# Where streamed weight tiles begin in their ring places: the 33 that began at the first byte now begin 192 bytes in

## The chip, the cores and the metric

The kernel runs on one core of one Trainium2 chip. The metric is the device time of one execution in microseconds (us); smaller is better. A trace of one execution, taken by the hardware profiler, stands beside the times.

## What is computed

A linear attention with an RMS norm, followed by a two-layer feed-forward net with an exact GELU, all in float32:

```python
kv  = einsum('bhsd,bhse->bhde', k, v)          # batch 8, heads 8, seq 576, head_dim 64
out = einsum('bhsd,bhde->bhse', q, kv)
x   = out / sqrt(mean(out*out, -1) + 1e-6) * g_norm     # then [4608 tokens, 512]
h   = x @ w_in                                  # 512 -> 2048
g   = 0.5 * h * (1 + erf(h / sqrt(2)))
y   = g @ w_out                                 # 2048 -> 512
```

## The kernel before

**Chunks.** The 4608 tokens are worked off in nine chunks `c` of 512. Chunks 0 and 1 are computed plainly (`layer1`, lines 665, and `layer2`, line 692). Chunks 2 to 8, about three quarters of the time, use a scheme with seven block products in place of eight (Winograd's form of Strassen's) for both layers; everything below is about these. Each float32 operand is split into a high and a low float32r part, and a product of 128 columns of weights is three TensorE instructions: high by high, low by high, high by low.

**Layer 1 of a chunk** (`product`, line 554). The chunk has eight column groups `j`, each with a first part (block products `k` = 0 to 3) and a second part (`k` = 4, 5, 6). One block product is 6 instructions. The weights are the stationary operand (loaded into the array by a weight load), the activations `x` the moving one, 256 columns wide. A weight tile holds two block products, so it serves 12 instructions. There are 336 instructions in layer 1 of a chunk. **Layer 2** (`Fast.matmuls`, line 1241) is 28 ticks `(k, n)` of 12 instructions, with the roles turned round: the weights move, the split GELU outputs are stationary.

**What interrupts layer 1.** TensorE's order is written out by hand. Between the parts of layer 1 it also works for the next chunk: the projections of the attention (line 241, `project_pair`), a folding of the squares (line 293, `fold`) and the sums over keys (line 188, `sum_kv`). In chunk 2 the projections come after the second parts of `j` = 0 and of `j` = 1. In chunks 3 to 7 they come after the first part of `j` = 0. The fold comes after the second part of `j` = 2, and in chunks 3 to 5 the sum over keys after the second part of `j` = 5 (in chunk 2 it lies in layer 2). After each of these interruptions layer 1 goes on with the first part of the next column group, whose first weight tile is `("in", j, 0)`. Chunk 8 has no next chunk and no interruption.

**The ring.** The split weight tiles of the scheme lie in HBM (`products`), 128 x 1024 float32 = 512 KB each. 301 uses of them over chunks 2 to 8 form a `queue`; the tiles that stay in SBUF (`RESIDENT`) are not in it. `fetch(n)` issues the DMA of the n-th use on SP's queue (line 507) into one of six places in turn, `RING` = `w_in0, 1, 2, 3, 10, 11`; `used` issues fetch n + 6 when TensorE has done with use n.

**Where a tile begins in its place.** A place is 4096 bytes a partition for the tile and 256 bytes more (`EXTRA`), so a tile can begin at the first byte or further in. `AWAY` is 48 float32 = 192 bytes. All tiles that stay in SBUF begin at `AWAY`. Of the ring's tiles, those for which `aligned` says yes begin at the first byte and all others at `AWAY`:

```python
away = 0 if aligned(*queue[n]) else AWAY
ring[n] = kept[i][:, away:away + 2 * DM]
```

Every SBUF tile from `x0` on (the moving operands `x`, the GELU outputs, the ring, the work tiles) has a size that is a multiple of 256 bytes, and they are allocated one behind the other. So all of them begin at the same remainder of 256 bytes: a ring tile at its first byte begins at the remainder of the operand that it is multiplied with, a tile at `AWAY` does not. Operands inside a tile begin at multiples of 512 bytes from its begin.

`aligned` says yes 33 times: in every chunk for the first tick of layer 2, `TICKS[0]`; for `("in", j, 0)` with `j` = 0, 2, 3, 4 in chunks 2 and 8, `j` = 0, 1, 4, 7 in chunks 3 to 5, `j` = 0, 1, 4 in chunks 6 and 7. In the words of the last paragraph but two: for the first tile of each layer, and for the first tile after each interruption of layer 1, but for the one in chunk 2 ahead of `j` = 1, where the last of layer 2 of chunk 1 (line 692) comes between; in chunk 8 the same four `j` as in chunk 2 are named.

Of the kernel before, what the change touches and what calls it, by code (L numbers as in the profile page):

```python
# [23 lines left out]
FAST = PLAIN  # L24
# [13 lines left out]
def linear_attn_rms_gelu_ffn(  # L38
# [18 lines left out]
    NT, DM = out.shape  # L57
    B, NP = kv_main.shape[:2]
# [5 lines left out]
    NCH = NT // CH  # L64
# [28 lines left out]
    AWAY = 3 * LINE  # L93
# [81 lines left out]
    def rows(r):  # L175
        return slice(r * D, (r + 1) * D)
# [209 lines left out]
    kept = {}  # L386

    def reused(i, dtype=F32):

        if i not in kept:  # L390
            kept[i] = block_tile(f"w_in{i}", dtype)
        return kept[i][:, :2 * DM]
# [77 lines left out]
    TICKS = [(0, 0), (0, 1), (0, 2), (2, 0), (2, 1), (0, 3), (2, 2), (2, 3)]  # L470
# [20 lines left out]
    queue = []  # L491
# [5 lines left out]
    ring = {}  # L497

    def fetch(n):

        if n < len(queue):
            key = queue[n][1]
            i = RING[n % len(RING)]
            reused(i, F32R)
            away = 0 if aligned(*queue[n]) else AWAY
            ring[n] = kept[i][:, away:away + 2 * DM]
            nc.sync.dma_start(out=ring[n].bitcast(F32), in_=products[key])

    def aligned(c, key):

        kind, j, k = key
        if kind == "out":
            return (j, k) == TICKS[0]
        if k:
            return False
        if c > FAST and c + 1 < NCH:
            return j in ((0, 1, 4, 7) if c + 2 < B else (0, 1, 4))
        return j in (0, 2, 3, 4)

    def operand(c, key):  # L520
        at = c, key
# [2 lines left out]
    def used(c, key):  # L524
        if (c, key) in place:
            n = place[c, key]
            ring.pop(n)
            fetch(n + len(RING))
# [254 lines left out]
    for d in range(0, 2 * D, BLK):  # L783
        h = d // D * D
        nc.gpsimd.tensor_tensor(
            out=fold[:, d:d + BLK], in0=ident[:, h:h + BLK], in1=ident[:, h + BLK:h + 2 * BLK],
# [27 lines left out]
    def sum_squares(n):  # L814
# [12 lines left out]
        out=half_g, in0=ps[:, :1], scalar1=0.5, scalar2=None, op0=ALU.mult  # L827
# [3 lines left out]
        out=sums[:, :P], lhsT=ones, rhs=eps, start=True, stop=False,  # L831
# [4 lines left out]
        out=root_g, in0=half_g, scalar1=D ** 0.5, scalar2=None, op0=ALU.mult  # L836
# [9 lines left out]
    for half in range(2):  # L846
# [6 lines left out]
        out=sums[:, :n_fold].rearrange("p (g b) -> p g b", g=2), lhsT=fold,  # L853
# [3 lines left out]
    for half in range(2):  # L857
        nc.scalar.activation(
            out=first.block((1, half)),
# [8 lines left out]
    for half in range(2):  # L868
# [3 lines left out]
            out=first.o_all[:, half], in0=first.ps.pop((0, half)), scalar=root_g, in1=bc,  # L872
            op0=ALU.mult, op1=ALU.mult,
        )
        n = 2 + half
        bc = bank(f"acc{n}")
        for t in range(NG):
            for h in range(2):
                at = column(n, t) + h
                nc.tensor.matmul(  # L880
                    out=bc[rows(h), t * P:(t + 1) * P],
# [173 lines left out]
    def later(c, i):  # L1055

        if i == 7:
            sums[c] = attn[c + 1].fold()
        if i in (5, 7):
            load_kv(c + 2, (i - 5) // 2)  # L1060
        if i == 9:
            attn[c + 2].load(0)
        if i == 10:
            attn[c + 2].load(1)
        if i in (5, 7):
            raw_out(6 + i // 7)
        if i == 15:
            place_kv(c + 2, range(NP))
        send()
        for n in {9: (0, 1), 14: (2, 3), 15: (4, 5)}.get(i, ()):  # L1070
            fetch(n)
        for n in {6: (0,), 9: (1,), 12: (2,), 14: (3,)}.get(i, ()):
            keep(RESIDENT[n])
# [43 lines left out]
    for s in range(PLAIN * NF):  # L1117
        c, i = divmod(s, NF)
# [5 lines left out]
        if c == 0:  # L1124
# [25 lines left out]
            for _ in range(2):  # L1150
                if i > 6 and RAW:
                    store_raw, j = RAW.pop(0)
# [8 lines left out]
        else:  # L1161
            spread_matmuls(c, i)
            g[s] = gelu(h.pop(s))
            nxt, k = attn[c + 1], SQUARES.index(i) if i in SQUARES else None
# [189 lines left out]
    for c in range(FAST, NCH):  # L1354
# [4 lines left out]
        for j, second in parts_of_layer1():  # L1359
# [26 lines left out]
            if waiting and (last or (j, second) != (waiting[0], True)):  # L1386
                n = waiting.pop(0) // 2
# [65 lines left out]
```

## Time and profile before

| | before |
|---|---|
| three runs | 776.0, 776.16, 777.76 us (median 776.16) |
| span of the profiled execution, first to last instruction | 774.5 us |
| TensorE (PE) busy | 767.6 us, 99% |
| VectorE (DVE), ScalarE (ACT), GpSimd (POOL) busy | 578.8, 360.4, 157.7 us |
| DMA | 244.89 MB, mean 316 GB/s |
| PE's granted clock | 0.999 |

The span is one execution under the profiler; the run's median lies 1.66 us above it, for what comes ahead of the first and behind the last instruction. In the lists of the profile, PE is a matmul instruction and PEld the weight load that goes with it. Matmuls overlap, since one is recorded as longer than the distance to the next, so a group's time is best taken from the start of its first instruction to the start of the next group's first. "x12" after a group is its number of instructions.

### The profile page before, as it was taken

To read this page: it belongs to the slowest core of one execution; us is meant where nothing else is said; L and a number is where in the kernel's file an instruction comes from. 1 tells how busy PE (TensorE), PEld (TensorE's weight loads), DVE (VectorE), ACT (ScalarE), POOL (GpSimd) and SP (SyncE) were. 2 spreads that over 40 slices of the span, in tenths; PEclk is the share of its full clock that TensorE was granted. 3 is DMA by queue.
4 is the path that set the end of the run, shared out by engine and by line. 5 is a ranking of instruction groups with operands and counts; after the bars stand their busy time and mean duration, and the time that the engine had idled before them with its cause. 6 is when DMAs were issued, how large, how long until landed. Compare 5 with 4: busy or idle time off the path is not lost.

```text
span 774.5 us, 16764 instructions
## 1 busy us (share of the span) xinstructions
PE 767.6 (99%) x6598; PEld 726.5 (94%) x6598; DVE 578.8 (75%) x1057; ACT 360.4 (47%) x689; POOL 157.7 (20%) x141
## 2 busy tenths in 40 slices
PE   8999999999999999999999999999999999999998
PEld 6888888888899999999999999999999999999998
DVE  3999987899668974789477947694689568964683
ACT  3777645534363644364334724462436353632460
POOL 1000145423527000610043002500160016001100
PEclk9999999999999999999999999999999999999999
DMA  9997966797999999979998999989898989799974
GB/s 343 406 408 255 334 227 227 241 357 263 337 312 353 374 339 348 372 266 353 349 356 298 320 376 332 335 276 346 306 328 281 346 302 325 243 329 339 331 244 168
DMA packets 89602, 244.89 MB, mean 316 GB/s; under 512 B 8884, under 2 KB 30900, under 8 KB 89524
## 3 DMA queue, kind: packets, MB, share of 16 engines
q1 hardware_dynamic: 89520, 243.83, 87.9%
q8 instruction: 52, 0.85, 0.4%
q14 instruction: 26, 0.21, 0.1%
q10 hardware_dynamic: 4, 0.00, 0.0%
HBM read 207.09 MB, written 34.08 MB: 311 GB/s over the span
## 4 chain that ended last, share of the span: by engine, by line
PE 95%; DMA 2%; DVE 2%; ACT 0%; SPq 0%; issue 0%
PE acc L1241 23%; PE acc L554 22%; PE h L554 13%; PE acc L692 11%; PE h L665 11%; PE a L1241 10%; PE a L188 2%; PE a L241 1%; DMA kv_main<-kv_main 1%; PE h L655 1%; DMA w_in<-qT 1%; PE acc L241 1%; DVE x L1219 1%; PE acc L880 0%; PE a L293 0%; DVE x L1208 0%
## 5 line engine op out<-in xcount | busy, mean ns | idle before, releaser
L665 PE MATMUL h<-x,w_in 128*128 128x512 f32 x360 | 87.0, 390 | 0.0
L665 PEld LDWEIGHTS h<-x,w_in 128*128 128x128 f32 x360 | 67.3, 188 | 14.4 <-ACT w_in L641 0.3
L692 PE MATMUL acc<-w_out,gh 128*128 128x512 f32 x256 | 79.6, 392 | 0.0
L554 PE MATMUL acc<-w_in,w_in 128*128 128x256 f32 x480 | 64.7, 278 | 0.0
L554 PEld LDWEIGHTS acc<-w_in,w_in 128*128 128x128 f32 x480 | 59.1, 188 | 0.3 <-issue 0.2
L692 PEld LDWEIGHTS acc<-w_out,gh 128*128 128x128 f32 x256 | 47.5, 188 | 10.2 <-issue 0.3
L554 PE MATMUL acc<-x,w_in 128*128 128x256 f32 x390 | 52.8, 279 | 0.0
L545 DVE TENSOR_TENSOR gl<-acc,gh 128x256 f32<-128x256 f32 (+1 forms) x77 | 34.4, 446 | 24.2 <-ACT gh L567 18.5
L692 PE MATMUL acc<-w_out,gl 128*128 128x512 f32 x128 | 49.8, 389 | 0.0
L554 PEld LDWEIGHTS acc<-x,w_in 128*128 128x128 f32 x390 | 48.1, 188 | 1.0 <-issue 0.8
L678 ACT ACTIVATE gh<-h 128x512 fp32r<-128x512 f32 x32 | 19.2, 599 | 63.0 <-PE h L665 63.0
L1241 PE MATMUL acc<-w_in,w_in 128*128 128x256 f32 x372 | 46.7, 277 | 0.0
L567 ACT COPY gh<-h 128x256 f32<-128x256 f32 x21 | 7.8, 369 | 81.7 <-PE h L554 81.7
L1241 PEld LDWEIGHTS acc<-w_in,w_in 128*128 128x128 f32 x372 | 44.4, 188 | 0.0
L1208 POOL TENSOR_TENSOR w_in<-w_in,w_in 128x512 f32<-128x512 f32 x5 | 6.5, 1298 | 181.5 <-ACT w_in L586 181.5
L1241 PE MATMUL acc<-w_in,x 128*128 128x256 f32 x324 | 40.6, 277 | 0.0
L334 POOL TENSOR_TENSOR o<-o,sq 128x512 f32<-128x512 f32 x24 | 33.3, 1386 | 35.2 <-DVE sq L338 34.3
L586 ACT ACTIVATE w_in<-acc 128x512 f32<-128x512 f32 x32 | 19.2, 599 | 44.0 <-DVE acc L545 44.0
L554 PE MATMUL h<-w_in,w_in 128*128 128x256 f32 x288 | 38.7, 277 | 0.0
L1241 PEld LDWEIGHTS acc<-w_in,x 128*128 128x128 f32 x324 | 38.6, 188 | 0.1
L283 DVE TRANSPOSE_TENSOR_REDUCE part<-sq 128x16 f32<-128x512 f32 x33 | 23.4, 708 | 17.1 <-ACT sq L273 17.1
L554 PEld LDWEIGHTS h<-w_in,w_in 128*128 128x128 f32 x288 | 35.5, 188 | 0.0
(302 smaller groups left out, 1911.2 us busy)
## 6 DMA issues: line engine op xcount, KB each, us to landing
w_in<-products_in SPq DMA_DIRECT2D x168, 512.0 KB, 5.3
w_in<-products_out SPq DMA_DIRECT2D x133, 512.0 KB, 5.1
products_in<-w_in SPq DMA_DIRECT2D x40, 256.0 KB, 3.9
w_in<-w_in SPq DMA_DIRECT2D x16, 512.0 KB, 10.2
kv_main<-kv_main SPq DMA_DIRECT2D x16, 512.0 KB, 6.4
w_out<-w_out SPq DMA_DIRECT2D x16, 512.0 KB, 10.2
q<-qT SPq DMA_DIRECT2D x15, 512.0 KB, 6.5
products_out<-w_out SPq DMA_DIRECT2D x23, 256.0 KB, 3.9
```

Of the source, the lines that this page charges most:

```text
L188: nc.tensor.matmul(out=ps[r, n * D:(n + 1) * D], lhsT=k[:, r], rhs=v[:, r], start=(j == 0), stop=(j == NJ),)
L241: nc.tensor.matmul(out=ps[rows(h), p % 2 * HALF + a:p % 2 * HALF + e], lhsT=kv[b % 2][rows(half), p, h ^ half], rhs=q[rows(half), h, a:e], ...
L283: nc.vector.tensor_reduce(out=self.part[:, 2 * k[0] + k[1], :], in_=sq.rearrange("p (b d) -> p b d", d=BLK), op=ALU.add, axis=AX.X, apply_ ...
L334: eng.tensor_tensor(out=o, in0=o, in1=bc, op=ALU.mult)
L545: return eng.tensor_tensor(out=out, in0=x, in1=y, op=op)
L554: nc.tensor.matmul(out=out, lhsT=y, rhs=x[:, z, kb], start=first and kb + i == 0, stop=kb == 1 and i == 2, skip_group_check=True,)
L567: nc.scalar.copy(out=u[:, left], in_=a[:, left])
L586: nc.scalar.activation(out=grid(t)[:, :, j % 2], in_=ps.rearrange("p (a n) -> p a n", a=2), func=AF.Gelu)
L665: nc.tensor.matmul(out=h, lhsT=parts["in", i][:, w][:, p * P:(p + 1) * P], rhs=at.x[p][:, x], start=(m + p == 0), stop=(m == 2 and p == NP ...
L678: nc.scalar.activation(out=gh, in_=h, func=AF.Gelu)
L692: nc.tensor.matmul(out=ps, lhsT=x[:, ts], rhs=parts["out", i][:, w], start=(i == 0 and m == 0), stop=(m == 2 and (i == NF - 1 or (i, t) == ...
L1241: nc.tensor.matmul(out=self.bank[name][a][:, a * HALF:(a + 1) * HALF], lhsT=x[:, at], rhs=y, start=(k in (0, 2, 1) and n + p + m == 0 and ...
```

## The change

All tiles of the ring begin at `AWAY`; the function `aligned` goes. The 33 transfers write, and the 396 instructions that read them (26 tiles in layer 1, 7 in layer 2, 12 each) read, 192 bytes further on. The order of instructions and their waits are the same on all engines; no instruction and no byte is added or taken away.

```diff
             key = queue[n][1]
             i = RING[n % len(RING)]
             reused(i, F32R)
-            away = 0 if aligned(*queue[n]) else AWAY
-            ring[n] = kept[i][:, away:away + 2 * DM]
+            ring[n] = kept[i][:, AWAY:AWAY + 2 * DM]
             nc.sync.dma_start(out=ring[n].bitcast(F32), in_=products[key])
-
-    def aligned(c, key):
-
-        kind, j, k = key
-        if kind == "out":
-            return (j, k) == TICKS[0]
-        if k:
-            return False
-        if c > FAST and c + 1 < NCH:
-            return j in ((0, 1, 4, 7) if c + 2 < B else (0, 1, 4))
-        return j in (0, 2, 3, 4)
```

## The prediction

> **What bounds the kernel now.** I read the page first, then the waits of TensorE, then its timeline where the seven-product chunks run.
>
> ```profile
> span 774.5 us, 16764 instructions
> PE   8999999999999999999999999999999999999998
> PEclk9999999999999999999999999999999999999999
> PE 95%; DMA 2%; DVE 2%; ACT 0%; SPq 0%; issue 0%
> ```
>
> TensorE is busy in every slice at an even clock, and 95% of the chain that ended last is its own work. Its waits, for the stretch from 207 to 771 us that holds chunks 2 to 8, come to one row:
>
> ```profile
> PE acc L1241 <- DVE x L1219: 0.2, 1, 0.2
> ```
>
> So TensorE waits for no weight tile, and the transfers have room: fetches are held back by TensorE, which has to free their places, not the reverse (below: the DMA queue's largest waits, then the landing times of line 507 as min/median/max).
>
> ```profile
> SPq L507 <- PE acc L554: 139.4, 105, 4.4
> ...
> DMA to landing us min/median/max: 3.0/5.2/8.2
> ```
>
> What is left is the distance from one matmul to the next. It isn't the same everywhere. This is the timeline of PE in layer 1 of chunk 2 (start, length, engine, line, operation):
>
> ```profile
> 212.34 0.39 PE L692 MATMUL acc<-w_out,gl 128*128 128x512 f32 x1
> 212.57 1.58 PE L554 MATMUL acc<-x,w_in 128*128 128x256 f32 x12
> 213.98 1.58 PE L554 MATMUL acc<-w_in,w_in 128*128 128x256 f32 x12
> 215.40 1.57 PE L554 MATMUL h<-w_in,w_in 128*128 128x256 f32 x12
> 216.81 0.86 PE L554 MATMUL h<-w_in,w_out 128*128 128x256 f32 x6
> 217.61 1.10 PE L241 MATMUL a<-q,kv 64*64 64x192 f32 x24
> 218.63 1.69 PE L554 MATMUL acc<-x,w_in 128*128 128x256 f32 x12
> 220.16 2.88 PE L554 MATMUL acc<-w_in,w_in 128*128 128x256 f32 x24
> 222.88 0.84 PE L554 MATMUL acc<-w_in,w_out 128*128 128x256 f32 x6
> ```
>
> From 220.16 to 222.88 us 24 matmuls take 2.72 us, 113.3 ns each; all their weights lie at 192 bytes. From 212.57 to 216.81 us 36 matmuls take 4.24 us, 117.8 ns each, and **their weights lie at 192 bytes too**. Between the two stand the projections and, at 218.63, a tile that begins at the first byte. The recorded durations (min/median/max) show the same three cases: first the stretch from 212.5 us, then that from 218.6 us.
>
> ```profile
> L554 PE MATMUL acc<-x,w_in x12: 279/279/280, 212.6 to 213.9; 128*128 128x256 f32 x12
> ...
> L554 PE MATMUL acc<-x,w_in x12: 278/282/386, 218.6 to 220.0; 128*128 128x256 f32 x12
> L554 PE MATMUL acc<-w_in,w_in x12: 276/276/276, 220.2 to 221.4; 128*128 128x256 f32 x12
> ```
>
> 276 ns belongs to the pace of 113.3 ns, 279 to 117.8, 282 to 283 to a tile at the first byte. What a tile at the first byte costs without an interruption ahead of it stands in chunk 8, which has none:
>
> ```profile
> 702.11 0.88 PE L554 MATMUL acc<-w_in,w_in 128*128 128x256 f32 x6
> 702.83 0.88 PE L554 MATMUL acc<-s,w_in 128*128 128x256 f32 x6
> 703.55 1.52 PE L554 MATMUL acc<-w_in,w_in 128*128 128x256 f32 x12
> ```
>
> 12 matmuls in 1.44 us, 120 ns each.
>
> So I read the trace thus: with weights at 192 bytes, layer 1 has two steady paces, 113.3 and 117.8 ns, and keeps the one that it is in: 42 matmuls in a row stayed slow, over four tiles. A tile at the first byte is slower than both, but the tile behind it comes out at 113.3. That is seen after all 26 such tiles of layer 1.
>
> **The change part by part.** No instruction, byte or wait moves; the terms are paces alone.
>
> *What it takes away.* A group of 12 at 120 ns instead of 113.3 is 12 x 6.7 ns = 0.08 us. I take that for the 7 of layer 2. Of the 26 in layer 1 most stand behind an interruption and start below 120 (at 218.63 the least is 278 and the median 282, not 283), so they are worth between 0.05 and 0.08 us; I take 0.065. For layer 2 the tile behind it also recovers slowly:
>
> ```profile
> 250.99 1.60 PE L1241 MATMUL acc<-w_in,w_in 128*128 128x256 f32 x12
> 252.43 1.54 PE L1241 MATMUL acc<-w_in,s 128*128 128x256 f32 x12
> 253.81 0.39 PE L1241 MATMUL acc<-r,x 128*128 128x256 f32 x2
> ```
>
> 1.44 us, then 1.38 where 12 x 113.3 is 1.36: 0.02 more, seven times. Together 26 x 0.065 + 7 x 0.08 + 0.14 = 2.4 us. This is the most that the change can gain.
>
> *What it may bring.* The tile at the first byte is also what stood behind each interruption of layer 1. Without it, the question is which pace layer 1 falls into there. The trace has one entry into layer 1 with no such tile, at 212.57, and it fell into 117.8. All the others have one. The bounds for each stretch from an interruption to the next are therefore 113.3 (all as after a first-byte tile) and 117.8 ns (as at 212.57). I take 117.8: it is the only row with the same weights, the same roles and no first-byte tile, though the work ahead of it was line 692 and not 241, 293 or 188. The stretches, by line 554 alone (length, PE busy, instructions; a count of 127 or 187 has one in it that ends there), are two of chunk 2 and its last, the three of chunk 3, two of chunk 7, and all of chunk 8:
>
> ```profile
> 218.62:223.64 5.02, 5.01 (x42) 1.00 0.90 322
> 224.68:229.62 4.94, 4.93 (x42) 1.00 0.85 284
> 229.75:250.98 21.23, 21.23 (x187) 1.00 0.95 344
> 297.18:311.64 14.46, 14.46 (x126) 1.00 0.86 317
> 311.77:326.29 14.52, 14.52 (x127) 1.00 1.00 369
> 328.78:335.75 6.97, 6.96 (x60) 1.00 0.76 251
> 620.56:635.02 14.46, 14.46 (x126) 1.00 0.85 292
> 635.15:656.38 21.23, 21.23 (x187) 1.00 0.93 325
> 694.56:732.94 38.38, 38.37 (x336) 1.00 0.92 336
> ```
>
> A stretch of n matmuls at 117.8 gains 12 x 2.2 = 0.03 us on the old first tile and loses (n - 12) x 4.5 ns on the rest. For n = 42 that is +0.11 us, for 60 +0.19, for 126 +0.49, for 186 +0.76. Chunk 2: 0.11 + 0.11 + 0.76 = 0.98. Chunks 3 to 5: (0.49 + 0.49 + 0.19) x 3 = 3.5. Chunks 6 and 7: (0.49 + 0.76) x 2 = 2.5. Sum +7.0 us.
>
> *Where a layer begins without an interruption.* Here the roles of the operands turn, and for one step a weight load and a moving operand lie at the same remainder, as inside a first-byte tile. In layer 2 the pace of 113.3 looks like the only one: it came back within a tile after 250.99, and also after an interruption with no first-byte tile, at 271.90:
>
> ```profile
> 271.28 0.69 PE L188 MATMUL a<-w_in 112*64 112x64 f32 x17
> 271.90 1.65 PE L1241 MATMUL acc<-w_in,x 128*128 128x256 f32 x12
> 273.38 1.52 PE L1241 MATMUL acc<-w_in,w_out 128*128 128x256 f32 x12
> 274.74 0.50 PE L1241 MATMUL acc<-w_out,w_out 128*128 128x256 f32 x3
> ```
>
> 1.48 us including the restart, then 1.36. So layer 2 saves its 0.56 + 0.14 = 0.70 us. For the begin of layer 1 (seven times) no row shows the case; a step at the same remainder is what led to 113.3 each time, so I take 113.3. With the three other tiles of chunk 8, ten tiles of layer 1 then save 10 x 0.065 = 0.65 us. If instead the begin falls into 117.8, chunks 3 to 7 lose little (24 matmuls to the first interruption, about 0.04 us each), but chunk 8 keeps it for 336 matmuls: 324 x 4.5 - 12 x 2.2 - 3 x 12 x 6.7 = 1.2 us lost instead of 0.3 gained.
>
> *Sum.* +7.0 - 0.70 - 0.65 = +5.65 us on the span of 774.5. The runs' median stands 1.66 us above the span, which the change doesn't touch: 776.16 + 5.65 = 781.8.
>
> *The row against the skill.* In the Trainium skill, the page "SBUF — State Buffer", section "Who interferes with whom", gives TensorE two independent read ports, one for the moving operand and one for weight loads, and says "PE and ACT never wait on anyone". By that rule 192 bytes would change no pace and the sum would be zero. The rows above disagree: 276 and 283 ns for the same instruction with the same operands' sizes, by the tile's begin.
>
> **The rivals.** A difference of 0.3%, 2.3 us, is about what a measurement of this kernel can tell from no change.
>
> 1. *Clean restart.* The slow stretch at 212.57 comes from line 692 ahead of it, and after lines 241, 293 and 188 layer 1 goes straight to 113.3, as layer 2 did at 271.90. Then only the first term is left: -2.4 us, 773.8. It decides at the first matmuls after each interruption. For it speaks the layer 2 row; against it that layer 2 recovered from everything and layer 1 stayed slow for 42 matmuls. Chance 0.13.
> 2. *Layer 1 slow from its begin as well*, chunk 8 above all: 1.5 us for chunk 8 and about 0.1 for each of six begins on top of the forecast, 784.0. No row shows this entry. Chance 0.22.
> 3. *Only one or two kinds of interruption lead to 117.8.* The projections' stretches (two of chunk 2, one in each of five chunks) are worth 0.22 + 5 x 0.49 = 2.7 us, the fold's 0.76 + 3 x 0.49 + 2 x 0.76 = 3.7, the sums' 0.6. With one of the two large ones alone, against the gains of 1.35 and of the clean stretches of some 0.6: +0.7 to +1.9 us, 776.9 to 778.1; the fold with the sums, or a slow pace that gets lost halfway, lie at 777 to 779. Chance 0.13.
> 4. *Layer 2 slow too*: (336 - 12) x 4.5 ns = 1.46 us in six chunks and some 0.7 in chunk 2, with the 0.70 not saved, on top of the forecast: 792. The recoveries at 252.43 and 271.90 speak against it. Chance 0.05.
> 5. *The begin is not what sets the pace.* If the 283 ns went with what runs beside these groups (DVE, DMA) and not with the address, nothing changes: 776.2. The groups at 702.11 have no interruption ahead of them and read other operands than those at 218.63, so little speaks for it. It is also what the Trainium skill's rule quoted above would give. Chance 0.04.
>
> **How the numbers follow.** The forecast has 0.43. Slower by over 0.3% are the forecast, rivals 2 and 4, and the upper part of 3 (0.06 of 0.13): 0.76. Within 0.3% are rival 5, the rest of 3 and half of rival 1, which ends right at the bound: 0.04 + 0.07 + 0.07 = 0.18. Faster is the other half of 1: 0.06. The range leaves out rivals 1 and 4 (0.18) and takes in 3 from its lower end and 2: 776.0 to 785.0, with 1 us above rival 2 for the spread of the runs.
>
> **What would show it.** In the profile after, groups of line 554 with recorded medians of 279 from each interruption to the next, 14.95 us in place of 14.46 for the 126 matmuls behind the projections of chunk 3, 22.0 in place of 21.23 for the 186 behind the fold of chunk 7, and no 282 or 283 anywhere in chunks 2 to 8. Layer 1 of chunk 8 takes 38.1 us if it begins well, 39.6 if not. Layer 2 has 276 from its second tile on. The forecast is wrong if the groups behind the interruptions show 276, if a slow stretch turns to 276 without an interruption, or if 279 stands in line 1241.

## The result, and the profile after

| | before | after |
|---|---|---|
| median of the runs | 776.16 us | 782.35 us |
| ratio, with 95% interval | | 1.0088 (1.0076 to 1.0099) |
| span of the profiled execution | 774.5 us | 782.6 us |

The change makes the kernel 0.9% slower by the ratio; the medians differ by 6.2 us. One of the five executions of the kernel before took 1290 us, and the ratio leaves it out. Of the 8.1 us between the two spans 1.5 lie ahead of chunk 2, where nothing is changed (PE's granted clock was 0.97 in the first 50 us of that execution); the spans of other executions of the kernel after are 780.5 to 781.6. The comparisons below go by stretches of chunks 2 to 8, which add up to +6.55 us.

TensorE is still busy throughout and the byte counts and instruction counts are the same. Lines have moved up by 12: layer 1 is now line 542, layer 2 line 1229.

```profile
span 782.6 us, 16764 instructions
PE   8999999999999999999999999999999999999998
PE 97%; DMA 2%; SPq 0%; DVE 0%; issue 0%
```

**Layer 1.** These are line 542's stretches in the profile after, in the order of the table in the prediction: three of chunk 2, three of chunk 3, two of chunk 7, chunk 8 (length, PE busy, instructions).

```profile
220.16:225.29 5.13, 5.13 (x42) 1.00 0.85 298
226.32:231.36 5.04, 5.03 (x42) 1.00 0.77 252
231.51:253.49 21.98, 21.98 (x187) 1.00 0.96 342
...
298.99:313.93 14.94, 14.93 (x126) 1.00 0.89 302
314.08:328.53 14.45, 14.45 (x127) 1.00 0.98 368
331.02:338.19 7.17, 7.16 (x60) 1.00 0.80 280
...
625.69:640.62 14.93, 14.93 (x126) 1.00 0.89 300
640.77:661.93 21.16, 21.16 (x187) 1.00 0.91 311
701.52:741.08 39.56, 39.56 (x336) 1.00 0.91 322
```

Behind the projections (298.99, 625.69) and the sums over keys (331.02) the time is what was forecast: 14.94 us where there were 14.46, 7.17 where there were 6.97. Behind the fold it is not: in chunk 2 (231.51) 21.98 us as forecast, but in chunks 3 and 7 (314.08, 640.77) 14.45 and 21.16, even less than before. And chunk 8 takes 39.56 us, the case of rival 2. The durations in two stretches of chunk 3, behind the projections and behind the fold:

```profile
L542 PE MATMUL acc<-x,w_in x15: 278/279/388, 299.0 to 301.5; 128*128 128x256 f32 x15
```
```profile
L542 PE MATMUL acc<-x,w_in x16: 276/276/363, 314.1 to 316.6; 128*128 128x256 f32 x16
```

279 ns against 276, the mark of the two paces.

**Layer 2.** Its seven chunks in the profile after; in chunk 2 up to the sum over keys, with the rest left out:

```profile
253.50:271.28 17.78, 17.77 (x156) 1.00 0.99 373
...
338.20:376.28 38.08, 38.08 (x336) 1.00 0.93 338
420.22:458.31 38.09, 38.08 (x336) 1.00 0.93 340
502.23:540.32 38.09, 38.08 (x336) 1.00 0.90 310
581.30:620.87 39.57, 39.56 (x336) 1.00 0.88 303
661.94:701.51 39.57, 39.56 (x336) 1.00 0.83 281
741.09:779.06 37.97, 37.96 (x335) 1.00 0.68 233
```

In chunks 3 to 5 and in 8 it is as the prediction had it. In **chunks 6 and 7 layer 2 is slow from end to end**, 39.57 us for 336 matmuls, 117.8 ns each. Before, it was 38.17 there; this is chunk 6:

```profile
577.62:615.79 38.17, 38.16 (x336) 1.00 0.91 314
```

In the profile after again, the durations at the begin of layer 2 of chunk 3 and of chunk 6:

```profile
L1229 PE MATMUL acc<-w_in,w_in x12: 276/276/286, 338.2 to 339.5; 128*128 128x256 f32 x12
```
```profile
L1229 PE MATMUL acc<-w_in,w_in x12: 281/281/283, 581.3 to 582.6; 128*128 128x256 f32 x12
```

So layer 2 has a slow pace too (recorded as 281 ns here), and it kept it for 336 matmuls. What differs is what came ahead. In chunks 2 to 5 and 8 layer 1 ended slow, and layer 2 ran at 113.3. In chunks 6 and 7 layer 1 ended at 113.3 (behind the fold, with no sum over keys after it), and layer 2 ran slow. In turn layer 1 began at 113.3 where the layer 2 ahead of it was at 113.3 (chunks 3 to 6), and slow where it was slow (chunks 7 and 8). That is the theory tested below: *each layer hands its pace to the next* (from layer 1 to layer 2 fast turns to slow and slow to fast, from layer 2 to layer 1 it stays), and a first-byte tile or an interruption is what breaks the chain.

### The profile page after: what moved, and what is told of

Same layout as the page of the kernel before. It is cut to its first block, busy times and chain, and to the rows that moved or that the text cites. A ratio compares the mean times of both kernels' runs of the same rounds, so it can differ in the third digit from the quotient of the medians.

```text
span 782.6 us, 16764 instructions
## 1 busy us (share of the span) xinstructions
PE 775.9 (99%) x6598; PEld 735.0 (94%) x6598; DVE 578.5 (74%) x1057; ACT 360.1 (46%) x689; POOL 157.4 (20%) x141
## 4 chain that ended last, share of the span: by engine, by line
PE 97%; DMA 2%; SPq 0%; DVE 0%; issue 0%
PE acc L1229 25%; PE acc L542 22%; PE h L542 13%; PE acc L680 11%; PE h L653 11%; PE a L1229 10%; PE a L188 2%; PE a L241 1%; DMA kv_main<-kv_main 1%; PE h L643 1%; DMA w_in<-qT 1%; PE acc L241 1%; PE acc L868 0%; PE a L293 0%; SPq L151 0%; DVE w L533 0%
```

## The experiments

The short diffs are against the kernel before. Ratios are to the kernel before, with 95% intervals.

**layer2_only.** One part of the change alone: the first tile of layer 2.

```diff
         if kind == "out":
-            return (j, k) == TICKS[0]
+            return False
```

> Only the first tile of layer 2 moves to 192 bytes; the 26 tiles of layer 1 stay at the first byte. Theory (the pace is handed from layer to layer: layer 1 ending at 113.3 ns puts layer 2 at 117.8, as in chunks 6 and 7 of the kernel after): every chunk's layer 2 is slow to its end or to the next stop, +1.4 us in six chunks and some 0.4 in chunk 2, about +9 us, 785: more than the whole change costs. Rival (layer 2 has one pace, as the prediction had it, and chunks 6 and 7 are slow for something in these chunks): -0.7 us, 775.5, or +2.5 if chunks 6 and 7 alone stay slow.

Measured: 784.14 us, ratio 1.0105 (1.009 to 1.012). A part of the change costs more than the whole: from the begin of layer 1 of chunk 2 to the end of the trace it is 8.4 us against 6.55 (by the medians 8.25 against 6.2). Layer 2 of chunks 3 to 8 (line 1241 here):

```profile
335.28:374.85 39.57, 39.56 (x336) 1.00 0.92 328
418.23:457.80 39.57, 39.56 (x336) 1.00 0.91 332
501.17:540.73 39.56, 39.56 (x336) 1.00 0.86 299
581.36:620.93 39.57, 39.56 (x336) 1.00 0.89 306
661.53:701.10 39.57, 39.56 (x336) 1.00 0.82 278
739.50:778.95 39.45, 39.45 (x335) 1.00 0.67 225
```

Here every layer 1 ends at 113.3, and layer 2 of chunks 3 to 8 runs at 117.8 from end to end. Layer 2 of chunk 2 begins at 117.8 as well; at 260.6 and 260.8 us two intervals of 194 and 223 ns break its stream, and from 261.5 us on it runs at 113.3. The rival, that chunks 6 and 7 are special, falls. So does the prediction's "one pace" for layer 2.

**layer1_only.** The other part: the 26 tiles of layer 1.

```diff
-        if k:
+        if kind == "in":
             return False
```

> Only the 26 tiles of layer 1 move to 192 bytes; the first tile of layer 2 stays at the first byte. Theory (handed on): layer 2 runs at 113.3 everywhere from its second tile on, so layer 1 begins at 113.3 in chunks 3 to 8, turns to 117.8 behind lines 241 and 188 and back behind the fold of chunks 3 to 7: +1.0 us in chunk 2, +0.6 each in chunks 3 to 5, +0.4 each in 6 and 7, -0.3 in chunk 8, together about +3, 779. Rival (each interruption leads to 117.8, as the prediction had it): +6.4, 782.5. Rival (chunk 8's layer 1 is slow whatever layer 2 did): +4.5, 780.7.

Measured: 778.41 us, ratio 1.0029 (1.0017 to 1.0041), near the 779 of the theory, 4.1 and 2.3 us below the rivals. Layer 1: of chunk 3 the three stretches behind an interruption, of chunk 4 the first two, and all of chunk 8:

```profile
296.81:311.74 14.93, 14.93 (x126) 1.00 0.84 299
311.89:326.34 14.45, 14.45 (x127) 1.00 0.95 373
328.83:336.00 7.17, 7.16 (x60) 1.00 0.83 270
...
378.92:393.86 14.94, 14.94 (x126) 1.00 0.86 294
394.01:408.69 14.68, 14.68 (x127) 1.00 0.98 360
...
696.92:734.99 38.07, 38.07 (x336) 1.00 0.95 336
```

Chunk 8 is at 113.3 from end to end, because layer 2 of chunk 7 was: the second rival of the expectation falls. The 14.68 in chunk 4 is neither 14.45 nor 14.94. The durations say why: up to 403.4 us they are 276, and from 403.8 us on 279.

```profile
L554 PE MATMUL acc<-w_in,w_out x5: 276/276/276, 402.9 to 403.4; 128*128 128x256 f32 x5
```
```profile
L554 PE MATMUL h<-w_out,w_in x5: 279/279/280, 403.8 to 404.3; 128*128 128x256 f32 x5
```

A single interval of 165 ns in place of 113, with no other matmul between, stands where layer 1 turned to the slow pace.

**away_256.** The 33 tiles begin 256 bytes in, the same remainder as the first byte.

```diff
-            away = 0 if aligned(*queue[n]) else AWAY
+            away = 4 * LINE if aligned(*queue[n]) else AWAY
```

> The 33 tiles begin 256 bytes into their places in place of the first byte, the others stay at 192. Theory (what counts is whether two operands that are read together lie at the same remainder of 256 bytes): the paces of before come back group for group, 282 to 283 in these 33 groups and 276 behind them, 776.2. Rival (it is the first byte of the place, or the transfer into it, that sets the pace anew): the slow stretches of the kernel after, 782.4.

Measured: 776.42 us, ratio 1.001 (1.0 to 1.002). The paces of before are back; so it is the remainder and not the first byte of the place. From chunk 8's layer 1, the second half of the first tile and the first half of the third (the tile between, from 695.98 to 697.34 us, took 113.3 ns a matmul):

```profile
L554 PE MATMUL h<-s,w_in x6: 280/283/283, 695.3 to 695.9; 128*128 128x256 f32 x6
L554 PE MATMUL acc<-w_in,w_in x6: 276/276/276, 697.3 to 697.9; 128*128 128x256 f32 x6
```

In this execution one stretch of chunk 2 broke the rule. There TensorE waited for a weight tile, and what followed ran at 279 ns until layer 2:

```profile
PE acc L554 <- DMA w_in<-products_in: 0.6, 1, 0.6
```
```profile
L554 PE MATMUL acc<-w_in,w_in x12: 279/279/355, 249.4 to 250.7; 128*128 128x256 f32 x12
```

That is a second break in the stream behind which layer 1 was slow. Not every break has this effect: in the same stretch, two intervals of 248 and 192 ns at 246.2 and 246.4 us left the pace at 113.3.

**all_128 and all_64.** Other shifts, with no tile at the first byte. The `AWAY` of the tiles that stay in SBUF changes as well.

```diff
-    AWAY = 3 * LINE
+    AWAY = 2 * LINE        # all_64: LINE
...
-            away = 0 if aligned(*queue[n]) else AWAY
+            away = AWAY
```

> All tiles of the ring and all that stay in SBUF begin 128 bytes into their places, none at the first byte. Theory A (192 bytes is 64 bytes short of the same remainder, near enough to collide in one of two phases; 128 is as far as can be): one pace, 113.3 throughout, 773.8. Theory B (any shift has two paces, picked at each stop): slow stretches as in the kernel after, 779 to 790. Should 128 bytes collide like the first byte, all of chunks 2 to 8 runs at 120: 805.

> All tiles of the ring and all that stay in SBUF begin 64 bytes into their places. Theory (the difference between the two operands counts, with its sign; layer 1 has now the difference that layer 2 had and the reverse): paces of 113.3 and 117.8 and no other, 774 to 790, with slow stretches where the kernel after has none. Rival (192 bytes is the one good shift, as 128 showed 118.7 and 120): 119 to 120 in all of chunks 2 to 8, 797 to 806.

all_128 took 798.88 us, ratio 1.0298 (1.0282 to 1.0313). There is no clean pace at 128 bytes: the recorded durations behind the projections and behind the fold of chunk 3 are

```profile
L554 PE MATMUL acc<-x,w_in x14: 279/281/285, 299.8 to 302.1; 128*128 128x256 f32 x14
```
```profile
L554 PE MATMUL acc<-x,w_in x15: 281/284/365, 314.4 to 316.9; 128*128 128x256 f32 x15
```

that is 118.7 and 120.0 ns from start to start. Theory A, that the farthest remainder would be clean, is wrong; B, two paces picked at each stop, holds in kind, but at other values, and its 779 to 790 us is missed. all_64 took 779.09 us, ratio 1.0042 (1.0028 to 1.0056), with the two paces 113.3 and 117.8 of the 192-byte shift, by and large with the roles of the layers swapped: a layer 2 at 113.3 now puts the next layer 1 at 117.8. From chunk 7's layer 2 to chunk 8's layer 1:

```profile
656.84:694.92 38.08, 38.07 (x336) 1.00 0.81 267
```
```profile
694.93:734.49 39.56, 39.56 (x336) 1.00 0.95 347
```

Not everything is swapped. Behind the projections layer 1 ran at 117.8 in chunks 2, 3 and 6, and it was at 113.3 after six matmuls in chunks 4, 5 and 7; here are chunks 3 and 4:

```profile
297.42:312.36 14.94, 14.94 (x126) 1.00 0.88 298
...
379.29:393.70 14.41, 14.40 (x126) 1.00 0.85 280
```

A shift of 192 bytes acts on a stationary tile by and large as one of 64 acts on a moving tile, and the reverse. The simplest reading is that the difference of the two remainders counts, with its sign: 64 bytes either way leaves a clean pace to be had, 0 and 128 do not. No run moved the other operand of the two, so the difference is told from the remainder of the shifted tile alone only by this swap.

**fold_ahead.** layer1_only, and a matmul of the fold's kind ahead of each restart behind lines 241 and 188 in chunks 3 to 7.

```diff
         a, b = (bank(n) for n in SETS[j % 3])
+        if at.c > FAST and at.c + 1 < NCH and (j == 1 or (j == NJ2 - 1 and at.c + 2 < B)):
+            nc.tensor.matmul(out=a[:, :64], lhsT=fold, rhs=heads[:, :64], start=True, stop=True)
```

> layer1_only, and one more matmul of the fold's kind (float32, 64 columns, into the bank that the next product overwrites, so no output depends on it) ahead of layer 1's restart behind lines 241 and 188 in chunks 3 to 7: eight of them, no tile moved. Theory (what the stream ran last before it restarts sets the pace, and the fold's kind of matmul leads to 113.3): the five stretches of 126 and the three of 60 turn from 117.8 to 113.3, -0.55 us and -0.27 us each, and eight extra matmuls cost 0.14 us each: 778.4 - 3.6 + 1.1 = 775.9. Rival (a stretch is slow for its place in the chunk, its tiles or its length): 778.4 + 1.1 = 779.5.

Measured: 783.7 us, ratio 1.0097 (1.0081 to 1.0113). The theory falls, and the rival's 779.5 is missed too: all eight stretches stayed slow, and four of the five folds of chunks 3 to 7, which had led to 113.3 without the added matmuls, now led to 117.8 as well, which cost 2.3 us in the trace against that of layer1_only. The eight added matmuls took 0.24 us each, not 0.14. Chunk 3, behind the added matmul and behind the fold:

```profile
299.56:314.47 14.91, 14.91 (x126) 1.00 0.89 300
314.62:329.63 15.01, 15.01 (x127) 1.00 0.99 384
```

So the fold's kind of matmul doesn't set a pace. Coming from the slow pace it can lead to either.

**picked.** First-byte tiles only where the kernel after turned slow, and one more ahead of `j` = 1 of chunk 2.

```diff
-        if c > FAST and c + 1 < NCH:
-            return j in ((0, 1, 4, 7) if c + 2 < B else (0, 1, 4))
-        return j in (0, 2, 3, 4)
+        if c == FAST:
+            return j < 5
+        return c + 1 < NCH and j in ((1, 7) if c + 2 < B else (1,))
```

> First-byte tiles only where the kernel after was slow and one more ahead of j = 1 of chunk 2: in chunk 2 j = 0 to 4, in chunks 3 to 5 j = 1 and 7, in 6 and 7 j = 1, and the first tile of layer 2 in all. Theory (a first-byte tile is needed only where the pace would turn to 117.8): 14 groups at 113.3 in place of 120 save 0.065 to 0.08 us each and the stretch at j = 1 of chunk 2 turns to 113.3, -1.1 us, 774.8. Should the fold lead to 117.8 where layer 1 comes to it at 113.3 (the kernel after only shows it from 117.8), the five stretches behind it lose 0.5 to 0.8 us each: 778.

Measured: 774.68 us against 775.72 of the kernel before beside it, ratio 0.9987 (0.9978 to 0.9996). It beats both kernels, by 0.13% and by some 1%. The first of these is small, but its interval leaves out 1, and in the traces the time from the begin of layer 1 of chunk 2 on is shorter by the same 1.0 us. The stretch of chunk 2 that was slow in both other kernels (5.03 us in the kernel after) takes 4.92 us, and all five folds, now met at 113.3, left it at 113.3 without a first-byte tile. The two rows are these:

```profile
211.85:216.77 4.92, 4.91 (x42) 1.00 0.97 347
...
310.86:325.31 14.45, 14.45 (x127) 1.00 0.98 378
```

**stop8_fold and stop8_64.** An interruption put into chunk 8 of picked, ahead of `j` = 4, where no other work of the next chunk runs.

```diff
         a, b = (bank(n) for n in SETS[j % 3])
+        if (at.c, j) == (NCH - 1, 4):        # stop8_fold
+            nc.tensor.matmul(out=a[:, :64], lhsT=fold, rhs=heads[:, :64], start=True, stop=True)
...
+            for r in range(4):               # stop8_64, in its place
+                nc.tensor.matmul(out=a[:D, :P], lhsT=heads[:D, :D], rhs=fold[:D], start=True, stop=True)
```

> picked, and in chunk 8, which has no interruption, one added matmul of the fold's kind (float32, 64 columns) ahead of the first part of j = 4; its output is overwritten. Layer 1 of chunk 8 comes to it at 113.3 ns. Theory (the fold's kind hands on the pace it meets if that is 113.3, as in all five folds of picked): the remaining 186 matmuls stay at 113.3, layer 1 takes 38.1 + 0.2 us. Rival (any interruption without a first-byte tile behind it leads to 117.8, as the prediction had it): 186 x 4.5 ns more, 39.1.

> picked, and in chunk 8 four added matmuls of the projections' kind (float32, 64 rows by 64, 128 columns wide) ahead of the first part of j = 4; their output is overwritten. Theory (interruptions by 64 x 64 float32 matmuls, lines 241 and 188, always lead to 117.8, whatever pace they meet and with no DMA or other engine about): layer 1 of chunk 8 turns to 117.8 there for 186 matmuls, 38.1 + 0.8 + some 0.6 for the added ones, 39.5. Rival (the pace behind lines 241 and 188 comes from what else runs in those parts of chunks 2 to 7): 38.7.

One execution each, 775.4 and 776.63 us (the kernel before beside them 776.26). The rest of layer 1 behind the added work, first stop8_fold, then stop8_64:

```profile
710.90:732.06 21.16, 21.16 (x187) 1.00 0.95 330
```
```profile
711.30:733.30 22.00, 22.00 (x186) 1.00 0.87 305
```

21.16 us is 186 matmuls at 113.3, 22.00 at 117.8. Both went by the theory, though the four matmuls added in stop8_64 took 1.0 us and not 0.6. So, coming from 113.3 with weights at 192 bytes, the added matmuls of 64 x 64 lead to 117.8 and the one of the fold's kind does not; no work for a next chunk is needed for it. Two things are not told apart. The added stops differ in length as well as in kind, 0.13 us and 1.0 us. And the weights went on streaming (a DMA share of 0.87 in the last row), against the words of the expectation that no DMA is about. Those words also call line 188 64 x 64; its matmuls are 112 x 64 and 128 x 64.

## Why the prediction was right, and where its sum was right by accident

- *TensorE is the bound and nothing waits for the shifted transfers*: right. No instruction of line 542 or 1229 waited in the profile after.
- *Layer 1 has two paces at 192 bytes, 113.3 and 117.8 ns, and keeps what it is in*: right, to the last digit. The first line of the sum's working, n matmuls at 117.8, gives 14.95, 7.16 and 22.0 us; 14.94, 7.17 and 21.98 were measured.
- *Interruptions by lines 241 and 188 lead to 117.8*: right in all ten of them in chunks 2 to 7, and in stop8_64. Forecast +2.67 and +0.57 us, measured +2.65 and +0.59.
- *The fold leads to 117.8*: right once in six, in chunk 2 (+0.76); in chunks 3 to 7 it led to 113.3, and the first-byte tile that had stood there was saved (5 x 0.06). Forecast +3.75 us, measured +0.46. This is the step of the working that failed first: the one row at 212.57 us was taken to hold for every kind of interruption.
- *Layer 2 has one pace, and saves 0.70 us*: wrong. Measured +1.82 us: two chunks slow, 1.40 each; the five others gained 0.09 or so each; and in chunk 2 another 0.56 us went with the wait for line 1219 and the break around it, for which the sum had no term. No trace in which layer 1 of chunk 2 takes at least 1 us longer shows that wait (this one, layer1_only, fold_ahead, away_256, all_128). The step that failed here is the reading of the recoveries at 250.99 and 271.90 as a sign of a single pace. Both entries come from a first-byte tile or from an interruption. What comes from a layer 1 at 113.3 had no row, and layer2_only shows that it leads to 117.8 each time, in all seven chunks.
- *Layer 1 begins at 113.3 where it is not interrupted*: right in chunks 3 to 6, where layer 2 ahead was at 113.3; wrong in chunk 2 (it comes from line 692, which had led to 117.8 in the row at 212.57) and in chunks 7 and 8, where layer 2 ahead was slow. Forecast -0.65 us, measured +1.03, nearly all of it chunk 8's +1.19. That was rival 2, and its price of 1.2 us was right.

Of the prediction's own signs of being wrong two came true: the groups behind five of the six folds show 276, and layer 2 of chunks 6 and 7 shows the slow pace. The third, a slow stretch that turns to 276 by itself, isn't in this trace.

The sum of the working was +5.65 us, and the stretches give +6.55. Three terms missed by -3.3, +2.5 and +1.7 and made up for each other. The sign rests on the part of the mechanism that was right, the two paces and lines 241 and 188. The size does not; that it came out is luck. By the hand-over that the runs showed, folds that lead to 117.8 would have left layer 2 and chunk 8 clean, and the sum would have come out nearly by its own terms (this is worked out, no run shows it); it came out by others. The rivals were priced as if independent; in fact a fold that leads to 113.3 (rival 3) is what brings the slow layer 2 (rival 4) and with it the slow chunk 8 (rival 2).

*Left open.* What a fold met at the slow pace decides by: it led to 113.3 in chunks 3 to 7 of the kernel after and to 117.8 in its chunk 2 and in most of fold_ahead, with the same operands' remainders. The intervals ahead of it differ by a few nanoseconds at most, about what the trace resolves. At a shift of 64 bytes the projections, too, led to either pace. Why the remainders matter, whether two reads collide as the expectations have it, and for how many bytes, is not shown; only that the pace goes with the remainders and with what ran before.

## What to carry to other kernels

When a profile shows one instruction with the same shape at two or three distinct durations, list them by operand addresses and by what ran ahead; a steady pace may be a state that the stream keeps, and then a change has to be priced by which state each restart leads to, not by the instructions that it touches. One row is not enough for that: each kind of entry needs its own. And where a deliberately slower step resets such a state, it is worth its cost only ahead of a stretch that would otherwise be slow: keeping 19 of the 33 and adding one made the best version here.

## What the runs showed of the hardware

- A stream of float32r matmuls, 128 x 128 weights and 256 columns, runs at 113.3, 117.8, 118.7 or 120.0 ns from start to start, depending on how far one operand's start address is shifted against the other's. Shift zero or 256 bytes: 120.0, seen over single tiles of 12 matmuls (before, away_256). 64 bytes either way (64 and 192): 113.3 or 117.8 (all_64, after). 128 bytes: 118.7 or 120.0 (all_128).
- The pace is kept over hundreds of matmuls (336 at 117.8 in one layer), over changes of tile and bank. It was changed by a tile at another remainder, by float32 matmuls with 64 columns of weights between (lines 241 and 188 ahead of layer 1, with weights at 192 bytes), by the exchange of the operands' roles, and at some breaks in the stream with no matmul between: in layer 1 one of 52 ns (layer1_only) and a wait of 0.6 us (away_256) led to 117.8, in layer 2 of chunk 2 one of layer2_only led to 113.3 and one of all_64 to 117.8. Other breaks left it as it was.
- The recorded duration of a matmul is a good mark of the pace, though the profile's legend says that the ends of matmuls are modelled: 276 ns goes with 113.3, 279 to 281 with 117.8, 283 and 284 with 120.0. A median of 281 alone is not enough, since it went with 118.7 in all_128 as well.
